# The tail of a cached attention: head 6 with V held still, head 5's sums and the last turn ahead of it, head 7 in steps

## The chip, the cores and the metric

The kernel runs on one core of a Trainium2 chip. The metric is the device time of one execution in microseconds. Times inside an execution are given in microseconds from the start of its span.

## The reference

Two layers of attention with a cached K and V, each followed by a gated feed-forward layer, for 4 sequences of one token each. The weights and the caches of both attention layers are the same; so are those of both feed-forward layers.

```python
# x [4,1,512]; k_cache, v_cache [4,8,8192,128]; wq [512,4096]; wo [4096,512]; bfloat16
def attention(x):                                   # 32 query heads over 8 K/V heads, W = 2048
    q = (x @ wq).reshape(B, 1, 32, 128).transpose(0, 2, 1, 3)
    k, v = (repeat(c[:, :, Sk - W:], 4, axis=1) for c in (k_cache, v_cache))
    p = softmax(einsum("bhqd,bhkd->bhqk", q, k) * 128 ** -0.5)
    o = einsum("bhqk,bhkd->bhqd", p, v)
    return o.transpose(0, 2, 1, 3).reshape(B, 1, 4096) @ wo
def feed_forward(x):                                # w_gate, w_up [512,1792], w_down [1792,512]
    return (sigmoid(x @ w_gate) * (x @ w_up)) @ w_down
x = x + attention(layernorm(x));  x = x + feed_forward(layernorm(x))
x = x + attention(layernorm(x));  x = x + feed_forward(layernorm(x))
```

"Head" below is one of the 8 K/V heads with its 4 query heads. Its V for the 4 sequences is 2 MB.

## The kernel before

**Plan and order.** The program is first a list of operations (`P.op`): each has an engine, an assumed duration, and tiles that it reads and writes. `_schedule` (L95) simulates all engines with those durations and picks an order for each engine; an operation's `odeps` only make it come later than certain others of its own engine in that order. SP's transfers keep the order of the list. Engines then run their lists in order, and wait on semaphores where tiles demand it. So an instruction that has to wait holds up everything behind it on its engine.

**The first half.** Attention 1 loads K and V head by head, turns K with TensorE and leaves it in SBUF (`kt`); output weights `wo` stay in `wo_sb`. A feed-forward layer follows.

**The second attention** is the loop over `HEADS2` (heads 0 to 7 in order). K lies in SBUF already; V is streamed again. `load_v` brings V of head n+2 into the place that K of head n left free, in one transfer for most heads and in three for head 7 (1 MB, 0.5 MB, 0.5 MB). Each step of the loop does `scores` for head n and then `v2_head` for head n-2 (`AHEAD = 2`); heads 6 and 7 come after the loop. For one head:

- `scores`: 16 products of q and K (L742), maximum (L751), its exchange between partitions (L755, L757, L761), exponential on ScalarE (L764), a 32x32 transpose on VectorE (L772) and the *turn*, one product with a permutation on TensorE (L775, named `PT`; the list `turns` keeps them).
- `weights`: the expansion of the turned exponentials into `pt` on VectorE (L786), the denominators (L798, L801 on VectorE, L806 on TensorE, reciprocal L811). `pt` has two halves, taken in turn.
- `pv_wo`: p times V, in one of two ways. Heads whose number is in `WIDE` take the *wide* way (`wide_pv`): pieces of `pt` are the stationary operand and V streams past in 32 products of 256 columns, four of them on different 32-column strips of the array (L827); ScalarE copies the four partial results out of PSUM (L835, named `pvc`), and matmuls in float32 add them up (L842, the head's *sums*). The others hold *V still*: 64 blocks of V of 128x128 are the stationary operand in turn, and 32 columns of `pt` stream past (L869). Then VectorE normalises (L879). For heads 0 to 6 there follow four *selection* matmuls (L905), a selection on VectorE (L912) and the head's *output projection* (L920, named `WO`), which adds into one PSUM bank over all seven heads. Head 7 has a projection of its own (L890).
- `early_residual` takes the seven heads' result out of PSUM: a cast on ScalarE (L932), the rest of it on VectorE (L935), and a turn on TensorE (L942, named `w_turn`).

In the second attention before the change, heads 0, 1 and 7 hold V still and heads 2 to 6 are wide; the exponential of head 7 is followed on ScalarE by the load of the table for the sigmoid (L766).

**The last feed-forward layer** (`glu`) has the layer norm, gate and up products (L1004), the sigmoid and the down-projection (56 products, L1072), whose result is copied (L1085) and sent out. Its weights are the last transfers of SP's list.

Of the kernel before, what the change touches and what calls it, by code (L numbers as in the profile page):

```python
# [267 lines left out]
def build(nc, A_x, A_k, A_v, A_wq, A_wo, B_wg, B_wu, B_wd, out):  # L268
# [4 lines left out]
    _, HKV, SK, DH = A_k.shape  # L273
# [28 lines left out]
    KLEAD = 3  # L302
    AHEAD = 2
    NWR = 7
    WIDE = {0: {0: 4, 1: 4, 2: 4, 3: 4, 4: 4, 5: 4, 6: 2}, 2: {2: 2, 3: 2, 4: 2, 5: 2, 6: 2}}
    HEADS1 = list(range(HKV))
    HEADS2 = list(range(HKV))

# [27 lines left out]
    with es:  # L336
# [54 lines left out]
        P = _Plan()  # L391


        def blk_ap(s):
            return {"kt": kt, "ar": arena, "pt": pt, "pb": pb, "sx": side}[s[0]][:, s[1] * UNIT:(s[1] + s[2]) * UNIT]

        def blk_tok(s):
            return tuple((s[0], u) for u in range(s[1], s[1] + s[2]))

        def kblk(h, b):  # L400
            return ("kt", (h * NB + b) * UBLK, UBLK)
# [9 lines left out]
        def ar(u, n):  # L411
            return ("ar", u, n)

        def sx(u, n):
            return ("sx", u, n)
# [23 lines left out]
        def c_dve(n, rate=None):  # L439
            return tm["dve_fix"] + n * (tm["dve_f32"] if rate is None else rate)  # L440

        def c_act(n):
            return tm["act_fix"] + n * tm["act_el"]
# [11 lines left out]
        def load_v(L, h):  # L455

            got = []
            u0 = 0
            for s in WHERE["V%d_%d" % (L, h)]:
                n = s[2]  # L460
                dma("V%d_%d_%d" % (L, h, u0), blk_ap(s), v_d[h][:, :, u0 * UNIT:(u0 + n) * UNIT], w=blk_tok(s),
                    rate={32: "bw_16k", 16: "bw_8k"}.get(n, "bw_4k"), nbytes=128 * n * UNIT * 2)
                got.append((s, u0 * UNIT // 128))
                u0 += n
            return got
# [267 lines left out]
        def scores(L, n, h, sbk, tbk):  # L733

            k2 = n % 2

            def e_s(pe):
                last = None
                for c in range(NCH):
                    for b in range(NB):  # L740
                        q0 = (h * NB + b) * STRIP + 28 - REP * c
                        last = pe.matmul(ps[32 * b:32 * b + 32, sbk, 0:CB * 128],  # L742
                                         qs[:, q0:q0 + 32],
                                         blk_ap(kblk(h, b))[:, c * CB * 128:(c + 1) * CB * 128],
                                         start=(c == 0), stop=(c == NCH - 1), skip_group_check=True)
                return last
            kr = [t for b in range(NB) for t in blk_tok(kblk(h, b))]
            P.op("tensor", "S%d_%d" % (L, h), 16 * tm["pe_s"] * (0.55 if L == 0 else 1.0), e_s, r=kr + [("qs",)], w=[("pss", sbk)], banks=(sbk,))
            nmv = nm[:, k2:k2 + 1]
            P.op("vector", "smax%d_%d" % (L, h), c_dve(CB * 128),  # L750
                 lambda v: v.tensor_reduce(nmv, ps[:, sbk, 0:CB * 128], AXX, ALU.max, negate=True),  # L751
                 r=[("pss", sbk)], w=[("nm", k2)], banks=(sbk,))

            P.op("vector", "sadd%d_%d" % (L, h), c_dve(32),
                 lambda v: v.tensor_scalar(tin[:, :], same[:, :], nmv, None, ALU.add),  # L755
                 r=[("nm", k2), ("same",)], w=[("tin",)])
            P.op("vector", "strn%d_%d" % (L, h), c_dve(32), lambda v: v.transpose(tout[:, :], tin[:, :]),  # L757
                 r=[("tin",)], w=[("tout",)])
            gv = nmg[:, k2:k2 + 1]
            P.op("vector", "smin%d_%d" % (L, h), c_dve(32),  # L760
                 lambda v: v.tensor_reduce(gv, tout[:, :], AXX, ALU.min), r=[("tout",)], w=[("nmg", k2)])  # L761
            zv = zz[:, k2:k2 + 1]
            def e_exp(a):
                o = a.activation(pbuf[:, :], ps[:, sbk, 0:CB * 128], ACTF.Exp, bias=gv, scale=1.0, accum_out=zv)  # L764
                if n == HKV - 1:
                    a.preload_act_table_set("sigmoid_and_others")  # L766
                return o
            P.op("scalar", "sexp%d_%d" % (L, h), c_act(CB * 128) + 200.0, e_exp,
                 r=[("pss", sbk), ("nmg", k2)], w=[("pb", 0), ("pb", 1), ("z", k2)], banks=(sbk,))


            P.op("vector", "ptr%d_%d" % (L, h), 650.0, lambda v: v.transpose(turned[:, :], pbuf[:, :]),  # L772
                 r=[("pb", 0), ("pb", 1)], w=[("pb", 2), ("pb", 3)])
            return P.op("tensor", "PT%d_%d" % (L, h), 270.0,
                 lambda pe: pe.matmul(ps[:, tbk, 0:CB * NQ].rearrange("p (j x) -> p j x", x=NCH * REP), perm[:, :],  # L775
                                      turned[:, :].rearrange("p (j x) -> p j x", x=32)[:, :, 0:NCH * REP],
                                      start=True, stop=True, skip_group_check=True),
                 r=[("pb", 2), ("pb", 3), ("perm",)], w=[("pspt", tbk)], banks=(tbk,))
# [70 lines left out]
        def pv_wo(L, n, h, pbk, pieces, prev=()):  # L849
            k2 = n % 2  # L850
            kp = n % NPT
            wide = WIDE[L].get(n, 0)
            obk = pbk[k2] if L else 6 if wide else 5
# [73 lines left out]
        def early_residual(L):  # L927


            hi, lo = pb[:, 0:D], pb[:, D:2 * D]  # L930
            tk = [("psw", n) for n in range(NWR)]
            P.op("scalar", "w_hi%d" % L, c_act(D), lambda a: a.copy(hi, ps[:, WB, 0:D]), r=tk, w=[("pb", 0), ("pb", 1)],  # L932
                 banks=(WB,))
            P.op("vector", "w_lo%d" % L, c_dve(D),
                 lambda v: v.tensor_tensor(lo, ps[:, WB, 0:D], hi, ALU.subtract),  # L935
                 r=tk + [("pb", 0), ("pb", 1)], w=[("pb", 2), ("pb", 3)], banks=(WB,))

            def e_turn(pe):
                last = None
                for c in range(NC):  # L940
                    for i, part in enumerate((hi, lo)):
                        last = pe.matmul(ps[:, MB, c * NB:(c + 1) * NB], part[:, c * 128:(c + 1) * 128], ofbb[:, :],  # L942
                                         start=(c == 0 and i == 0), stop=(i == 1), skip_group_check=True)
                return last
            P.op("tensor", "w_turn%d" % L, 8 * tm["pe_pair"], e_turn,
                 r=[("pb", u) for u in range(4)] + [("ofbb",)], w=[("pswt",)], banks=(MB,))
            P.op("vector", "w_early%d" % L, c_dve(NX),
                 lambda v: v.tensor_tensor(xT[:, :], ps[:, MB, 0:NX], xT[:, :], ALU.add),
                 r=[("pswt",), ("xT",)], w=[("xT",)], banks=(MB,))
# [144 lines left out]
        def eyes(L, at, kinds):  # L1094

            got, a0 = {}, 0
            for wide in kinds:
                rows = NR * wide
                e_ = blk_ap(at)[:, a0:a0 + 2 * rows].bitcast(F32)
                P.op("vector", "eye%d_%d" % (L, rows), c_dve(128),  # L1100
                     lambda v, e_=e_, rows=rows: v.tensor_reduce(
                         e_, ident_b[:, :].rearrange("p (q y) -> p y q", y=rows), AXX, ALU.add),
                     r=[("ident_b",)], w=list(blk_tok(at)) if a0 == 0 else [("eye", L, rows)])
                got[wide] = e_
                a0 += 2 * rows
            SUMS[L, "eye"] = (tuple(blk_tok(at)) + tuple(("eye", L, NR * w_) for w_ in kinds[1:]), got)

        layer_norm(0, SCALE)
        eyes(0, ar(40, 1), sorted(set(WIDE[0].values())))

# [54 lines left out]
        vs2 = {}  # L1165
        SB2, TB2 = [3, 0], [1, 2]

        def v2_head(n):
            h = HEADS2[n]
            if n == min(WIDE[2], default=-1):  # L1170
                eyes(2, sx(20, 1), sorted(set(WIDE[2].values())))
            if n == NWR:
                early_residual(2)
            pv_wo(2, n, h, (5, 6), vs2[h], turns[n + 1:n + 2])

        for n in range(2):
            vs2[HEADS2[n]] = load_v(2, HEADS2[n])
        turns = []
        for n, h in enumerate(HEADS2):
            turns.append(scores(2, n, h, SB2[n % 2], TB2[n % 2]))  # L1180
            if n + 2 < HKV:
                vs2[HEADS2[n + 2]] = load_v(2, HEADS2[n + 2])
            if n >= AHEAD:
                v2_head(n - AHEAD)
            weights(2, n, h, TB2[n % 2])
        for n in range(HKV - AHEAD, HKV):
            v2_head(n)
# [62 lines left out]
```

## Time and profile before

| | us |
|---|---|
| median of 3 runs (lowest to highest) | 180.2 (179.79 to 180.32) |
| the profiled execution: its own time | 179.77 |
| its span | 177.7 |
| TensorE busy, weight loads | 130.0, 94.6 |
| VectorE, ScalarE, GpSimd busy | 104.4, 64.4, 6.5 |
| 70.31 MB of transfers, mean rate over the span | 396 GB/s |
| mean granted TensorE clock | 0.831 of full |
| last of K's scores (L742, head 7) ends | 152.37 |
| head 5's products (L827) | 153.76 to 154.82 |
| V of head 6 lands | 158.40 |
| head 6's products (L827) | 158.44 to 160.20 |
| head 6's output projection (L920) starts | 164.73 |
| x after the second attention (L542) | 167.66 |
| down-projection (L1072) starts | 173.51 |

The columns of a view are named ahead of it. PE is TensorE, PEld its weight loads (which overlap with products), DVE VectorE, ACT ScalarE, POOL GpSimd, SP the engine that issues transfers; a "q" behind an engine's name is its sequencer. "x" is a count. A name such as `ps<-kt,pt` gives what is written and what is read; in `128*32 128x256` the first pair is rows and columns of the array that the stationary operand fills, the second the operand that streams past. Brackets at a line's end hold the idle time of the engine ahead of it and what ended it. The busy time of TensorE in products is modelled at their ends.

### The profile page before, as it was taken

What the parts mean: (1) busy time and instruction counts of PE and PEld (TensorE: products, weight loads), DVE (VectorE), ACT (ScalarE), POOL (GpSimd) and SP (SyncE); (2) the same over time, 40 slices, a digit from 0 to 9 for tenths busy, and PEclk for the clock granted to TensorE, in tenths of its full rate; (3) what the DMA queues carried; (4) which work ended last, traced back from release to release, by engine and by line L of the source; (5) the groups of instructions that cost most, each with busy time, mean ns of one, the idle gap of its engine ahead of it and who ended that gap; (6) DMA issues with size and microseconds to landing.
All of it is one profiled execution on the core that took longest, in us unless ns stands there. A gap on an engine that the chain in (4) does not pass through costs nothing.

```text
span 177.7 us, 4796 instructions
## 1 busy us (share of the span) xinstructions
PE 130.0 (73%) x2139; PEld 94.6 (53%) x2139; DVE 104.4 (59%) x271; ACT 64.4 (36%) x94; POOL 6.5 (4%) x16
## 2 busy tenths in 40 slices
PE   0494399898895986968867767658757966748883
PEld 0382198666482663745735457648215744436673
DVE  7443016989668385786767452113599997834440
ACT  2073207966385571875642510300031132150100
POOL 5200000000000000000000001002000000000020
PEclk9999657999999999999999555555699999985555
DMA  5999999999999999999999999999999999999940
GB/s 196 420 419 424 422 443 417 435 409 437 420 424 420 423 432 424 420 428 410 422 432 388 405 407 404 368 366 410 418 445 420 424 435 428 422 407 405 411 178 5
DMA packets 10369, 70.31 MB, mean 396 GB/s; under 512 B 1129, under 2 KB 1901, under 8 KB 6893
## 3 DMA queue, kind: packets, MB, share of 16 engines
q1 hardware_dynamic: 10340, 70.00, 95.3%
q8 instruction: 17, 0.28, 0.6%
q14 instruction: 4, 0.02, 0.0%
q10 hardware_dynamic: 8, 0.00, 0.0%
HBM read 70.00 MB, written 0.00 MB: 394 GB/s over the span
## 4 chain that ended last, share of the span: by engine, by line
DMA 59%; PE 17%; DVE 9%; SPq 6%; issue 4%; ACT 3%; POOLq 1%; POOL 0%; ACTq 0%; DVEq 0%
DMA arena<-in_A_v_cache_dram 43%; DMA kt<-in_A_v_cache_dram 12%; SPq L448 6%; DMA arena<-in_A_wq_dram 5%; PE ps L827 4%; PE ps L742 2%; PE ps L1004 2%; DVE pt L786 2%; PE ps L842 2%; ACT pb L764 1%; DVE nmz L751 1%; PE ps L869 1%; PE ps L1072 1%; PE ps L920 1%; DVE pb L772 1%
## 5 line engine op out<-in xcount | busy, mean ns | idle before, releaser
L729 ACT COPY kt<-ps 128x1024 bf16<-128x1024 bf16 x40 | 39.5, 1013 | 22.1 <-PE ps L719 21.8
L719 PE MATMUL ps<-ident_r,kt 128*128 128x128 bf16 x512 | 38.6, 232 | 3.4 <-DMA kt<-in_A_k_cache_dram 2.7
L719 PEld LDWEIGHTS ps<-ident_r,kt 128*128 128x128 bf16 x512 | 33.2, 106 | 10.4 <-issue 3.3
L729 DVE COPY kt<-ps 128x1024 bf16<-128x1024 bf16 x24 | 29.2, 1217 | 10.2 <-PE ps L719 10.2
L764 ACT ACTIVATE pb<-ps,nmz 128x512 bf16<-128x512 f32 x16 | 11.0, 689 | 36.2 <-DVE nmz L761 36.2
L786 DVE TENSOR_TENSOR pt<-ps,ofbr 128x1024 bf16<-128x1024 f32 x16 | 19.4, 1212 | 2.6 <-PE ps L775 2.6
L742 PE MATMUL ps<-kt,qs 128*32 128x512 bf16 x256 | 17.9, 407 | 4.1 <-ACT pb L764 2.8
L772 DVE STREAM_TRANSPOSE pb<-pb 128x512 bf16<-128x512 bf16 x16 | 11.3, 705 | 13.1 <-ACT pb L764 13.0
L827 PE MATMUL ps<-arena,pt 128*64 128x512 bf16 (+1 forms) x128 | 13.4, 391 | 7.0 <-DMA arena<-in_A_v_cache_dram 7.0
L751 DVE TENSOR_REDUCE nmz<-ps 128x1 f32<-128x512 f32 x16 | 10.9, 683 | 4.4 <-PE ps L742 4.4
L827 PEld LDWEIGHTS ps<-arena,pt 128*64 128x64 bf16 (+1 forms) x128 | 6.0, 117 | 12.3 <-DMA arena<-in_A_v_cache_dram 8.3
L742 PEld LDWEIGHTS ps<-kt,qs 128*32 128x32 bf16 x256 | 5.9, 101 | 10.5 <-ACT pb L764 3.6
L835 ACT COPY arena<-ps 128x512 f32<-128x512 f32 (+1 forms) x7 | 3.9, 556 | 13.4 <-PE ps L827 13.4
L842 PE MATMUL ps<-arena 128*128 128x16 f32 x52 | 7.3, 272 | 1.7 <-ACT arena L835 1.2
L612 POOL TENSOR_TENSOR rs<-pt,rs 128x4 f32<-128x4 f32 x4 | 4.0, 1012 | 120.3 <-DVE pt L608 120.3
L1004 PE MATMUL ps<-xn,arena 128*128 128x5 bf16 (+1 forms) x210 | 7.6, 172 | 0.8 <-DVE pt L600 0.6
L1004 PEld LDWEIGHTS ps<-xn,arena 128*128 128x128 bf16 x210 | 7.7, 118 | 1.0 <-issue 0.6
L842 PEld LDWEIGHTS ps<-arena 128*128 128x128 f32 x52 | 6.7, 201 | 2.5 <-ACT arena L835 2.5
L920 PE MATMUL ps<-wo_sb,onr 128*16 128x512 bf16 x56 | 6.4, 445 | 1.7 <-DVE onr L912 1.7
L827 PE MATMUL ps<-kt,pt 128*32 128x256 bf16 x160 | 6.0, 298 | 1.9 <-DMA kt<-in_A_v_cache_dram 1.9
L660 DVE TENSOR_TENSOR qs<-ps,rs 128x64 bf16<-128x64 f32 x2 | 0.4, 220 | 10.0 <-PE ps L650 10.0
L775 PE MATMUL ps<-pb,perm 128*128 128x256 bf16 x16 | 4.7, 293 | 1.9 <-DVE pb L772 1.8
(122 smaller groups left out, 144.2 us busy)
## 6 DMA issues: line engine op xcount, KB each, us to landing
kt<-in_A_k_cache_dram SPq DMA_DIRECT2D x8, 2048.0 KB, 24.5
arena<-in_A_v_cache_dram SPq DMA_DIRECT2D x7, 2048.0 KB, 20.1
kt<-in_A_v_cache_dram SPq DMA_DIRECT2D x5, 2048.0 KB, 18.0
wo_sb<-in_A_wo_dram SPq DMA_DIRECT2D x8, 512.0 KB, 25.1
arena<-in_B_w_gate_dram SPq DMA_DIRECT2D x6, 448.0 KB, 7.8
arena<-in_B_w_up_dram SPq DMA_DIRECT2D x5, 448.0 KB, 6.9
kt<-in_A_wq_dram SPq DMA_DIRECT2D x2, 1024.0 KB, 10.0
arena<-in_B_w_down_dram SPq DMA_DIRECT2D x4, 512.0 KB, 13.4
```

Source lines behind the costliest of these rows:

```text
L448: o = P.op("sync", name, 0.0, lambda e, dst=dst, src=src: e.dma_start(dst, src), r=r, w=w, dma_bytes=nbytes, dma_rate=tm[rate])
L719: last = pe.transpose(bankb(bank)[:, (v * NB + q) * 128:(v * NB + q + 1) * 128], kt[:, c0:c0 + 128], ident_b[:, :])
L729: return (e.tensor_copy if ev == "vector" else e.copy)(to, fr)
L742: last = pe.matmul(ps[32 * b:32 * b + 32, sbk, 0:CB * 128], qs[:, q0:q0 + 32], blk_ap(kblk(h, b))[:, c * CB * 128:(c + 1) * CB * 128], sta ...
L751: lambda v: v.tensor_reduce(nmv, ps[:, sbk, 0:CB * 128], AXX, ALU.max, negate=True),
L764: o = a.activation(pbuf[:, :], ps[:, sbk, 0:CB * 128], ACTF.Exp, bias=gv, scale=1.0, accum_out=zv)
L772: P.op("vector", "ptr%d_%d" % (L, h), 650.0, lambda v: v.transpose(turned[:, :], pbuf[:, :]), r=[("pb", 0), ("pb", 1)], w=[("pb", 2), ("pb ...
L786: lambda v: v.tensor_tensor(ptv.rearrange("p (j b r) -> p j b r", b=NB, r=REP), ps[:, tbk, 0:CB * NQ].rearrange("p (j r) -> p j r", r=REP) ...
L827: last = pe.matmul(ps[rows * g:rows * (g + 1), bank, 0:wide * 128].rearrange("p (c d) -> p c d", c=wide), pt[:, w0:w0 + rows], v, start=(i ...
L842: last = pe.matmul(ps[:, out[0], out[1]:out[1] + NR], part[:, c * 128:(c + 1) * 128], ey[wide][:, c * NR:(c + 1) * NR], start=(c == 0), st ...
L920: last = pe.matmul(ps[32 * j:32 * j + NR, WB, 0:D], onr[:, j * NR:(j + 1) * NR], wo_sb[:, h * WOH + j * D:h * WOH + (j + 1) * D], start=(n ...
L1004: last = pe.matmul(ps[:, bank, fc * wid:(fc + 1) * wid], cols[:, fc - g0, :], xn[:, ktc * (NB + 1):ktc * (NB + 1) + wid], start=(ktc == 0 ...
```

## The change

Head 6 leaves `WIDE` and so holds V still. Three lists are kept beside the loop: `turns` as before, `exps` (the exponential of each head) and `worked` (the output projection of the head handled last). With them, four orders are added:

- head 7's exponential comes after head 5's `pvc` on ScalarE;
- head 6's products come after head 5's output projection on TensorE, and after the last turn as before;
- of head 7's three pieces, the first comes after head 6's selection matmuls and the second after head 6's output projection;
- head 7's own projection comes after `w_turn`.

```diff
-    WIDE = {0: {0: 4, 1: 4, 2: 4, 3: 4, 4: 4, 5: 4, 6: 2}, 2: {2: 2, 3: 2, 4: 2, 5: 2, 6: 2}}
+    WIDE = {0: {0: 4, 1: 4, 2: 4, 3: 4, 4: 4, 5: 4, 6: 2}, 2: {2: 2, 3: 2, 4: 2, 5: 2}}
...
             if n == NWR:
                 early_residual(2)
-            pv_wo(2, n, h, (5, 6), vs2[h], turns[n + 1:n + 2])
+            n0 = len(P.ops)
+            pv_wo(2, n, h, (5, 6), vs2[h], turns[n + 1:n + 2] + worked if n == HKV - AHEAD else turns[n + 1:n + 2])
+            new = P.ops[n0:]
+            worked[:] = [o for o in new if o.name.startswith("WO")]
+            if n == HKV - AHEAD - 1:
+                exps[-1].odeps.update(o for o in new if o.name.startswith("pvc"))
+            if n == HKV - 1:
+                mine = [o for o in new if o.name.startswith(("PV", "WO"))]
+                for name, o in (("sel2_%d" % HEADS2[n - 1], mine[0]), ("WO2_%d" % HEADS2[n - 1], mine[1]), ("w_turn2", mine[-1])):
+                    o.odeps.update(p for p in P.ops if p.name == name)
...
-        turns = []
+        turns, exps, worked = [], [], []
         for n, h in enumerate(HEADS2):
             turns.append(scores(2, n, h, SB2[n % 2], TB2[n % 2]))
+            exps.append(P.ops[-3])
```

The order that results at the end of the second attention, on TensorE from head 4's output projection on:

| before | after |
|---|---|
| products of head 6 (32 wide) | sums of head 5 |
| last turn | last turn |
| sums of head 5 | selection of head 5 |
| sums of head 6 | output projection of head 5 |
| selection of head 5, denominators of head 7 | denominators of head 7 |
| selection of head 6 | products of head 6 (64, V still) |
| output projection of head 5 | selection of head 6 |
| products of head 7, first half | products of head 7, first half |
| output projection of head 6 | output projection of head 6 |
| products of head 7, second half | products of head 7, second half |
| `w_turn`, projection of head 7 | `w_turn`, projection of head 7 |

On VectorE, behind the transpose L772 of head 7: before, L798 and L801, the expansion L786, then L879 of heads 5 and 6, L912 of head 5, L811, L912 of head 6; after, L879 of head 5, L798, the expansion L786, L912 of head 5, L801, L811, L879 and L912 of head 6. The orders on SP and GpSimd are the same.

## The prediction

> **What bounds the kernel now.** I read the slices of the page first, then the chain of waits from 150 us on, the timeline around the changed steps, the windows of TensorE's clock, the source view of the narrow products, and the DMA issues. The slices give busy tenths in 40 equal parts of the span (4.44 us each):
>
> ```profile
> PE   0494399898895986968867767658757966748883
> PEclk9999657999999999999999555555699999985555
> DMA  5999999999999999999999999999999999999940
> ```
>
> The transfers never pause until slice 38, so nothing that ends inside the stream is worth time by itself. What counts is what ends after the stream: slices 38 and 39. The chain (start us, us, what) says which work that is:
>
> ```profile
> 137.76 20.64 DMA kt<-in_A_v_cache_dram
> 158.44 1.76 PE ps L827 x32
> 160.21 0.33 PE ps L775
> 160.53 0.68 PE ps L842 x4
> 161.24 0.38 ACT side L835
> 161.66 1.05 PE ps L842 x4
> 162.74 0.21 DVE onb L879
> ...
> 163.83 0.97 PE ps L869 x32
> 164.80 0.56 PE ps L920 x3
> 165.39 0.59 ACT pb L932
> ...
> 167.66 0.19 DVE xn L542
> ```
>
> From the landing of head 6's V at 158.40 on, the chain holds no transfer: it is compute alone, down to the output at 175.24. Head 6's wide products come first (L827), then three pieces of older work that stand in TensorE's queue behind them: the last turn (L775), head 5's sums (first L842), and only then head 6's sums (second L842). The timeline shows why head 5's sums are so late:
>
> ```profile
> 156.84 1.28 ACT L766 ACT_TABLE_LOAD   x1
> 158.14 0.37 ACT L835 COPY side<-ps 128x256 f32<-128x256 f32 x1
> 160.57 1.23 DVE L786 TENSOR_TENSOR pt<-ps,ofbr 128x1024 bf16<-128x1024 f32 x1 [2.62 <-PE ps L775]
> 163.76 1.03 PE L869 MATMUL ps<-pt,kt 128*128 128x32 bf16 x32
> ```
>
> The 158.14 copy is head 5's; its products ended at 154.82, but it stood behind the last exponential and the table load. TensorE meanwhile sat idle, and its clock was halved just as the last stretch began (columns: busy and count of PE, PEld, DVE, ACT, POOL, then PEclk, DMA share, GB/s):
>
> ```profile
> 157.00:158.00 1.00, 0.00 (x0) 0.00 (x0) 0.92 (x3) 1.00 (x1) 0.00 (x0) 1.00 1.01 422
> 159.00:160.00 1.00, 1.00 (x24) 0.59 (x16) 0.00 (x0) 0.00 (x0) 0.00 (x0) 0.50 1.03 418
> ```
>
> **The change, part by part**, on the clock of the profiled execution (span 177.7, its own time 179.77, so 2.07 outside the span; the median of the runs is 180.2, 0.43 above it). Per engine the order of instructions is unchanged up to head 4's output projection on TensorE (ends 156.53). No transfer is moved: SP issues the same list, its last weight load at 158.45, and GpSimd's list is unchanged.
>
> Head 5's copy before the last exponential: it may run at 154.87 to 155.24 (0.37). The exponential waits for L761 until 155.95 and started at 156.05, so the move costs nothing while those 0.7 us of cover last, 0.37 if they did not.
>
> Head 5's sums before the last turn: 156.53 to 157.05 (0.52, the 153.31 row at full clock). The turn waits for VectorE's transpose, which ends 157.57. Free, and the 0.68 after 160.53 goes.
>
> The last turn: 157.62 to 157.90 (0.28, as at 153.19) instead of 160.14. VectorE takes head 5's normalising (0.18) behind the transpose, then the expansion L786 at 157.93 to 159.15 (1.23), and only then head 5's selection L912, 159.06 to 159.27. This is the added wait. Head 5's output projection (L920) needs that selection: 159.32. Behind it in TensorE's queue stand the last denominators (L806) and all of head 6's products. A projection at half clock holds the next matmul 0.53 (163.23 to 163.76), the denominators another 0.14 (140.28 to 140.42). So head 6's products start at 159.32 + 0.53 + 0.14 = 159.99, 1.55 later than before, though V landed at 158.40.
>
> Head 6 with V still: 32 wide products (1.76), a copy (0.38) and its sums (1.05) go; 64 narrow ones come. Their row:
>
> ```profile
> L869 PEld LDWEIGHTS ps<-pt,kt x64: 103/104/115, 163.8 to 166.1; 128*128 128x128 bf16 x64
> L869 PE MATMUL ps<-pt,kt x64: 187/188/208, 163.8 to 166.1; 128*128 128x32 bf16 x64
> ```
>
> 32 of them took 1.03 with 0.188 for one, hence (1.03 - 0.188)/31 = 27 ns apart at half clock; at full clock (38 in 1.10, one 0.176) 25 ns. So 64 take 0.188 + 63 x 0.027 = 1.90: they end at 161.89. Normalising (0.04 to start, 0.18) ends 162.11; the selection matmuls start 162.16 and hold the next 0.24 (162.99 to 163.23): head 7's first half starts 162.40 (its V landed at 142.82 + 18.1 = 160.92), and head 6's projection 0.97 later, 163.37; before it was 164.73. VectorE's selection for it is done by 162.8. The sum is **164.73 - 163.37 = 1.36 us**.
>
> Behind it nothing changes shape: cast L932, difference L935, turn L942, head 7's projection L890, x at about 166.3. Head 7's second half starts at 163.9; its last V piece landed at 144.05 + 19.4 = 163.45 and is needed at 164.3, a cover of 0.85. The turn ahead of head 7's projection is the order they already had. The layer norm, GLU and down-projection move up whole: the down-projection would start at 172.15, and its four weights landed at 169.1, 170.4, 171.6 and
>
> ```profile
> arena<-in_B_w_down_dram SPq DMA_DIRECT2D x1, 256.0 KB, 13.8
> ```
>
> that is 158.45 + 13.8 = 172.25, needed by the last 8 of 56 products, near 173.4. So the whole 1.36 reaches the end.
>
> One correction. The clock changed at 18.69, 28.93, 97.19, 127.91 and 158.63 us: the distances are 3, 20, 9 and 9 times 3.413 us, so it is decided on a fixed raster whose phase each run draws anew. The window that ended at 158.63 held 0.94 us of PE busy. Other phases put the fall anywhere from about 157 to 160.2. Later than 158.6 it favours the kernel before: with its wide products at 1.06 (row 153.76) instead of 1.76 and head 5's sums at 0.52, it wins up to 1.05, the changed kernel only some 0.25 (one projection), because the narrow products hardly feel the clock. The gain is then 0.56 to 1.36 over the late half of the phases and about 1.3 over the early half. I take **1.2 us**: 180.2 - 1.2 = 179.0 (178.6 on the profiled execution's own time).
>
> **The rivals.** *The clock stays up* (faster still). The steps pulled forward fill the idle stretch from 156.5 to 158.4: sums 0.52, turn 0.28, selection 0.3. PE busy in that window would rise from 0.94 to about 1.8; the window from 127.92 had 1.74 and kept the clock. Then everything after runs at full clock and only the last weights bound the end: last products at about 172.6 rather than 175.2, a gain of 2.6, so 177.6. Against it: the window from 93.79 held 2.38 busy and still lost the clock, so busy time is not what is counted, and these steps are short streams of 16 columns. The Trainium skill, "TensorE: Matmul & The Clock Gate", section "The HAM clock gate", has a free-running window of about 3.4 us and lets an idle one halve the clock; the raster here agrees (3.413 us), but the window that lost it was not idle. By that rule, taken strictly, this rival would win.
>
> *The fall comes late in the usual run of before* (slower). If the clock held until 162.05, the wide path would put head 6's projection at about 162.8, ending 163.2, against 163.97 for the changed kernel at half clock: its start on the narrow products comes 1.5 late and is not won back. It is 0.6 to 0.8 slower: about 180.8. It decides once before keeps full clock past about 161.5. Against it: such a run of before would be some 2 us shorter than the profiled one, while the timed runs lie at 179.79 to 180.32 around 179.77.
>
> *Weight loads do not hide behind the narrow products* (slower). Each of the 64 loads takes 104 ns; end to end they would be 6.7 instead of 1.90, 4.8 more: 180.2 - 1.2 + 4.8 = 183.8. It decides from a spacing of about 27 + 1360/64 = 48 ns. The row of head 7 speaks against it: 27 ns apart, with the same shape, in the same place. The Trainium skill, "TensorE: Matmul & The Clock Gate", section "Packing small matmuls", says that a load overlaps with matmuls in flight only where its row group differs, which speaks against V held still, since all these loads fill all 128 rows; the trace here does not agree, 32 pairs of 104 and 188 ns having taken 1.03 us.
>
> *A transfer ends last* (no change). If the runs' transfers end later than the profile's by some 2.4 us, the last weights bound both kernels and the reordering is hidden: 179.9 to 180.4. The median's 0.43 above the profile is for it; that the weights lay ready before 173.5 is against it. Between 1.2 and 2.4 later it hides part.
>
> **How the numbers follow.** A difference of about 0.3%, 0.54 us, is what a measurement of this kernel can tell from none. Forecast, a gain of 0.6 to 1.7 (178.5 to 179.6): 0.68. Clock stays up (177.6): 0.06. Transfers hide it (179.9 to 180.4): 0.12. Late fall (180.8): 0.11. Loads bare (183.8): 0.03. Faster is 0.68 + 0.06 = 0.74, same 0.12, slower 0.14. The range takes in the forecast and the no-change case, and at the low end 0.3 us more for narrow products at 25 ns and a projection at full clock: 178.2 to 180.4.
>
> **What the next profile would show.** Right: head 5's copy near 154.9 ahead of the exponential; its sums near 156.5; 64 narrow products starting near 160.0, not at V's landing, ending near 161.9; head 6's projection near 163.4; x near 166.3; the clock at half from about 158.6. Wrong would be: narrow products more than 35 ns apart, a wait for V of head 7 at 163 to 165, a wait for down-projection weights after 172, or full clock beyond 162 in either kernel.

## The result, and the profile after

The changed kernel takes 178.75 us (median of 6 runs, 178.44 to 179.13); before takes 180.25 beside it (6 runs, 179.79 to 180.58). The ratio is 0.9922 with a 95% interval of 0.9902 to 0.9941: 1.1 to 1.8 us less. The forecast was 179.0, or 1.2 us less. The profiled execution took 178.58, with a span of 176.6.

The chain of waits after (start us, us, what), from head 7's exponential to x:

```profile
156.45 0.79 ACT pb L764 x2
157.26 0.72 DVE pb L772
158.03 0.30 PE ps L775
158.35 1.22 DVE pt L786
159.57 0.14 DVE onr L912
159.76 0.61 PE ps L920 x3
160.37 0.15 PE ps L806 x2
160.52 1.74 PE ps L869 x64
162.28 0.20 DVE onb L879
...
162.84 0.87 PE ps L869 x32
163.71 0.56 PE ps L920 x4
164.30 0.59 ACT pb L932
...
166.56 0.19 DVE xn L542
```

Before, the chain came out of a transfer at 158.40. Now no transfer is on it: head 6's V is there, and its 64 products stand behind the last turn, the expansion (L786), head 5's selection and projection. Between them and head 6's projection (163.64) stand the normalising, head 6's selection and the first half of head 7; the copy and the two rounds of sums that stood there before are gone. The timeline shows head 5's copy and sums where the change put them, in time in which TensorE had waited:

```profile
155.34 0.37 ACT L835 COPY side<-ps 128x256 f32<-128x256 f32 x1 [2.48 <-PE ps L827]
...
156.92 0.62 PE L842 MATMUL ps<-side 128*128 128x16 f32 x4
...
160.38 1.87 PE L869 MATMUL ps<-pt,kt 128*128 128x32 bf16 x64
```

One thing moves against the change in this execution: at 131.82 to 135.24 the clock was halved for one stretch of the raster, in a part that is the same in both kernels, and everything behind it is 0.4 later than in the profile of before (the last exponential at 156.45 instead of 156.05). Measured from that exponential, head 6's projection comes 7.19 us after it instead of 8.68: 1.49 less.

### The profile page after: what moved, and what is told of

The parts are those of the page before. It is cut to its first block, busy times and chain, and to the rows that moved or that the text cites. A ratio compares the mean times of both kernels' runs of the same rounds, so it can differ in the third digit from the quotient of the medians.

```text
span 176.6 us, 4850 instructions
## 1 busy us (share of the span) xinstructions
PE 129.3 (73%) x2167; PEld 94.5 (53%) x2167; DVE 104.7 (59%) x271; ACT 64.2 (36%) x93; POOL 6.5 (4%) x16
## 4 chain that ended last, share of the span: by engine, by line
DMA 52%; DVE 18%; PE 18%; ACT 5%; issue 3%; SPq 2%; POOLq 1%; POOL 0%; ACTq 0%; DVEq 0%
DMA arena<-in_A_v_cache_dram 31%; DMA kt<-in_A_k_cache_dram 11%; DVE pt L786 5%; DMA arena<-in_A_wq_dram 5%; DMA arena<-in_B_w_up_dram 4%; PE ps L719 4%; PE ps L827 4%; PE ps L742 3%; ACT pb L764 3%; DVE pb L772 3%; DVE nmz L751 2%; PE ps L869 2%; SPq L448 2%; DVE tout L757 1%; PE ps L1072 1%
## 5 line engine op out<-in xcount | busy, mean ns | idle before, releaser
L719 PE MATMUL ps<-ident_r,kt 128*128 128x128 bf16 x512 | 39.4, 235 | 4.4 <-DMA kt<-in_A_k_cache_dram 3.7
L719 PEld LDWEIGHTS ps<-ident_r,kt 128*128 128x128 bf16 x512 | 33.8, 107 | 11.5 <-DMA kt<-in_A_k_cache_dram 4.1
L742 PE MATMUL ps<-kt,qs 128*32 128x512 bf16 x256 | 19.0, 427 | 3.8 <-ACT pb L764 2.5
L786 DVE TENSOR_TENSOR pt<-ps,ofbr 128x1024 bf16<-128x1024 f32 x16 | 19.4, 1215 | 0.2 <-PE ps L775 0.2
L772 DVE STREAM_TRANSPOSE pb<-pb 128x512 bf16<-128x512 bf16 x16 | 11.3, 709 | 13.1 <-ACT pb L764 13.0
L827 PE MATMUL ps<-arena,pt 128*64 128x512 bf16 (+1 forms) x128 | 12.6, 355 | 7.1 <-DMA arena<-in_A_v_cache_dram 7.1
L842 PE MATMUL ps<-arena 128*128 128x16 f32 x52 | 7.2, 269 | 2.7 <-ACT arena L835 2.2
L842 PEld LDWEIGHTS ps<-arena 128*128 128x128 f32 x52 | 6.6, 197 | 3.5 <-ACT arena L835 3.5
L561 PE MATMUL ps<-pt,nmz 128*128 128x4 f32 x12 | 3.5, 362 | 3.4 <-DVE pt L583 2.5
L806 PE MATMUL ps<-zd,rqb 128*128 128x16 bf16 x32 | 3.3, 176 | 3.4 <-DVE pt L786 3.3
```

What stands on the lines that cost most here:

```text
L719: last = pe.transpose(bankb(bank)[:, (v * NB + q) * 128:(v * NB + q + 1) * 128], kt[:, c0:c0 + 128], ident_b[:, :])
L742: last = pe.matmul(ps[32 * b:32 * b + 32, sbk, 0:CB * 128], qs[:, q0:q0 + 32], blk_ap(kblk(h, b))[:, c * CB * 128:(c + 1) * CB * 128], sta ...
L786: lambda v: v.tensor_tensor(ptv.rearrange("p (j b r) -> p j b r", b=NB, r=REP), ps[:, tbk, 0:CB * NQ].rearrange("p (j r) -> p j r", r=REP) ...
L827: last = pe.matmul(ps[rows * g:rows * (g + 1), bank, 0:wide * 128].rearrange("p (c d) -> p c d", c=wide), pt[:, w0:w0 + rows], v, start=(i ...
L842: last = pe.matmul(ps[:, out[0], out[1]:out[1] + NR], part[:, c * 128:(c + 1) * 128], ey[wide][:, c * NR:(c + 1) * NR], start=(c == 0), st ...
```

## The experiments

They ran in turns with the kernel before, in three groups (e1 to e4, e5 to e8, e9 to e11), each group on a chip of its own. The ratio is to before; it is not exactly the ratio of the two medians. Before, head 6's projection starts 8.68 us behind head 7's last exponential, after it 7.19; I give this distance for each, because it leaves out shifts that come from earlier stages (it still depends on when the clock fell in that one execution: for e10 the clock was full from 155.49 to 165.73, so that its 5.21 cannot be set beside e3's 6.33).

| run | median us | before | ratio (95%) | exponential to head 6's projection |
|---|---|---|---|---|
| e1: orders, head 6 wide | 179.18 | 180.07 | 0.9943 (0.9915 to 0.9970) | 7.63 |
| e2: still alone | 178.92 | 180.07 | 0.9948 (0.9925 to 0.9972) | 7.48 |
| e3: products not held behind projection | 177.99 | 180.07 | 0.9895 (0.9864 to 0.9927) | 6.33 |
| e4: selection first | 178.32 | 180.07 | 0.9913 (0.9882 to 0.9944) | 6.67 |
| e5: copy not first | 180.32 | 179.97 | 1.0039 (1.0014 to 1.0065) | 8.89 |
| e6: no steps | 178.62 | 179.97 | 0.9938 (0.9911 to 0.9964) | 7.07 |
| e7: before with filler | 178.66 | 179.97 | 0.9933 (0.9905 to 0.9960) | 6.59 |
| e8: after with filler | 178.25 | 179.97 | 0.9920 (0.9895 to 0.9946) | 6.77 |
| e9: after again | 179.02 | 180.09 | 0.9945 (0.9925 to 0.9965) | 6.93 |
| e10: as e3, again | 178.48 | 180.09 | 0.9903 (0.9872 to 0.9935) | 5.21 |
| e11: as e3, last piece split | 177.86 | 180.09 | 0.9880 (0.9846 to 0.9913) | 6.20 |

**e1, the orders with head 6 still wide.** The changed kernel with

```diff
-    WIDE = {0: {0: 4, 1: 4, 2: 4, 3: 4, 4: 4, 5: 4, 6: 2}, 2: {2: 2, 3: 2, 4: 2, 5: 2}}
+    WIDE = {0: {0: 4, 1: 4, 2: 4, 3: 4, 4: 4, 5: 4, 6: 2}, 2: {2: 2, 3: 2, 4: 2, 5: 2, 6: 2}}
```

> All the added orders, but head 6 stays wide (its wide products cannot be held behind head 5's projection, so they start at the landing of V). Theory A (work queued between V's landing and head 6's projection is what the change shortens): head 5's copy leaves ScalarE early, its sums (0.68 us after the landing in the trace of before) lie before the landing, and head 6's copy no longer waits for them; head 6's sums start near 160.7 instead of 161.66, its projection near 163.7 instead of 164.73: about 1.0 us less than before, 179.2. Rival B (holding V still is what gains, since the copy and the float32 sums of head 6 go): no gain, 180.2. Rival C (filling TensorE's idle stretch keeps its clock up): full clock in the tail and up to 2.6 us less, 177.6.

1.0 us less, as theory A has it. The timeline of TensorE:

```profile
159.01 1.17 PE L827 MATMUL ps<-kt,pt 128*32 128x256 bf16 x32 [1.93 <-DMA kt<-in_A_v_cache_dram]
160.11 0.39 PE L775 MATMUL ps<-pb,perm 128*128 128x256 bf16 x1
...
160.65 1.03 PE L842 MATMUL ps<-side 128*128 128x16 f32 x4
...
163.62 0.60 PE L920 MATMUL ps<-wo_sb,onr 128*16 128x512 bf16 x4
```

Behind the landing there is one round of sums (L842) instead of two. So most of the gain can be had without holding V still; the runs do not tell e1 from the changed kernel. In this execution the clock fell only at 159.82, so its wide products took 1.17 instead of 1.76 and part of what the trace shows is that.

**e2, V still and no order.** The kernel before with the first line of the change alone.

> Only head 6 leaves the wide way, none of the orders. Theory A: head 5's copy still waits behind the last exponential and the table load (158.1 to 158.5); its sums, now ahead of the last turn and of head 6's products in TensorE's queue, hold these until about 160.2; head 6's projection starts near 163.9 instead of 164.73: 0.8 us less than before, 179.4, and 0.6 more than the changed kernel. Rival B: all of the gain is here, 178.75.

0.94 us less than before; its interval overlaps the changed kernel's. By the times alone rival B is not excluded: its 178.75 is nearer to the median than theory A's 179.4, and e9 below, the changed kernel again, gains no more (0.9945). Against B stand e1, which gained with head 6 wide, and the trace: head 5's sums came at 159.10, after a wait for the copy, and held up the rest until 160.57, as theory A says.

```profile
159.10 1.03 PE L842 MATMUL ps<-side 128*128 128x16 f32 x4 [2.03 <-ACT side L835]
...
160.57 1.87 PE L869 MATMUL ps<-pt,kt 128*128 128x32 bf16 x64
```

Either half thus gives about 1 us, and both together 1.4 in the first comparison and 1.0 in the second (e9), less than the 2.0 of the halves added: the two seem to take away the same wait in part. That both give more than either alone is not shown.

**e3 and e10, head 6's products not behind head 5's projection.** The changed kernel with

```diff
-            pv_wo(2, n, h, (5, 6), vs2[h], turns[n + 1:n + 2] + worked if n == HKV - AHEAD else turns[n + 1:n + 2])
+            pv_wo(2, n, h, (5, 6), vs2[h], turns[n + 1:n + 2])
```

> The changed kernel without one of its orders: head 6's products need not come after head 5's projection; they then stand right behind the last turn and head 5's selection. Theory A (in the changed kernel these products wait for VectorE's expansion, 1.5 us after V landed): they start at the landing, near 158.4 on the scale of before; head 6's projection near 162.1; the landing of head 7's last piece (163.45) is the next bound, x near 165.0 instead of 166.1: 1.1 us less than the changed kernel, 177.6. Rival: V of head 6 or 7, or the last weights (172.25), bound the tail already, so nothing is won, 178.7.

> The changed kernel without the order of head 6's products behind head 5's projection, again: 0.5 to 1.1 us less than the changed kernel on the same chip. Rival (the earlier difference was the spread of the runs): within 0.3 of it.

0.9895 and 0.9903 of before; on the same chip as the second, the changed kernel (e9) had 0.9945:

> The changed kernel again, unaltered, to stand on one chip beside the two that follow: about 1.4 us less than before, 178.7.

The difference of e9 and e10 is 0.0042 of 180 us, 0.8 us (0.5 by the medians), inside what was expected, but the two intervals still overlap a little (0.9925 to 0.9965 and 0.9872 to 0.9935). TensorE's timeline of e3 shows the wait gone, and the next one:

```profile
159.36 1.89 PE L869 MATMUL ps<-pt,kt 128*128 128x32 bf16 x64 [0.75 <-DMA kt<-in_A_v_cache_dram]
161.18 0.60 PE L920 MATMUL ps<-wo_sb,onr 128*16 128x512 bf16 x4
...
162.87 0.60 PE L920 MATMUL ps<-wo_sb,onr 128*16 128x512 bf16 x4
...
164.42 0.56 PE L869 MATMUL ps<-pt,kt 128*128 128x32 bf16 x16 [0.41 <-DMA kt<-in_A_v_cache_dram]
```

The products start at V's landing, head 5's projection follows them, and the last 16 products of head 7 wait for its last piece. Of the four orders that the change adds, this one seems to be a cost.

**e4, head 5's selection ahead of the expansion.** The changed kernel with, behind the loop,

```diff
+for o in P.ops:
+    if o.name == "ptx2_7":
+        o.odeps.update(p for p in P.ops if p.name in ("osel2_5",))
```

> The changed kernel with one order more: on VectorE head 5's selection comes ahead of the expansion for head 7, so that head 5's projection can run near 158.4 instead of 159.3, and head 6's products start near 158.9 to 159.0 instead of 160.0. Theory A: again bounded by head 7's last piece at 163.45; about 1.0 us less than the changed kernel, 177.7. Rival as for the run without the order: 178.7. A second rival: the expansion, 0.4 later, becomes the wait of head 7's products; it is not needed before 161, so no cost is expected.

178.32, ratio 0.9913: the direction expected, between theory A's 177.7 and its rival's 178.7, with a size that the runs cannot tell from none against the changed kernel (intervals overlap). Its runs spread from 177.18 to 179.82, and the profiled one is the longest: there the clock fell at 151.58 and stayed at half to the end (e10's fell at 152.08 but came back at 155.49), and head 5's wide products took 1.90 (155.06 to 156.96) instead of 1.06.

**e5, the copy not ahead of the exponential.** The changed kernel without `exps[-1].odeps.update(...)`.

> The changed kernel without one order: head 5's copy may stay behind head 7's exponential and the table load on ScalarE. Theory A: the copy then ends near 158.5, head 5's sums near 159.5, the last turn near 159.9, the expansion near 161.1; head 5's projection, and with it head 6's products that are ordered behind it, start near 161.4 and 162.0 instead of 159.3 and 160.0: 1.5 to 2 us more than the changed kernel, 180.2 to 180.8, no gain or a loss against before. Rival: the copy is a detail and the gain stays, 178.8.

180.32: 0.3 to 1.2 us *more* than before. The timeline has the chain that was expected, each step 0.6 to 1 later on the clock of this execution:

```profile
159.12 0.37 ACT L835 COPY side<-ps 128x256 f32<-128x256 f32 x1
...
159.55 0.88 PE L842 MATMUL ps<-side 128*128 128x16 f32 x4 [2.03 <-ACT side L835]
...
160.68 1.22 DVE L786 TENSOR_TENSOR pt<-ps,ofbr 128x1024 bf16<-128x1024 f32 x1
...
161.82 0.21 DVE L912 TENSOR_TENSOR onr<-ps,ofbr 128x64 bf16<-128x64 f32 x1
...
162.11 0.60 PE L920 MATMUL ps<-wo_sb,onr 128*16 128x512 bf16 x4
```

So the orders on TensorE pay with the copy early and not with it late. With it late, e2 gained and e5 lost; beyond e2, e5 has the order of head 6's products behind head 5's projection and the steps of head 7, and e6, which follows, shows no effect of the steps. That points to that order as what turns the change into a loss.

**e6, without the steps of head 7.** The changed kernel without the block under `if n == HKV - 1`.

> The changed kernel without the orders on head 7's pieces and on its projection: three quarters of head 7's products then precede head 6's projection, whose cast and difference therefore start about 0.3 later, but head 7's own projection runs before the turn instead of behind it, which takes 0.3 to 0.5 off the end. Theory A: within 0.4 of the changed kernel, 178.4 to 179.1. Rival: the steps carry a good part of the gain, 179.4 or more.

178.62 and 0.9938, no different from the changed kernel (0.9922 and 0.9945). Head 6's projection ended 163.90 and head 7's own was over at 165.24, before the turn ended at 165.74. Neither a gain nor a loss by the steps shows.

**e7 and e8, a filler for the clock.** Products of `ident_b` with `wo_sb[:, 0:512]` into a PSUM bank that is not in use, whose results nobody reads:

```diff
+            def e_warm(pe):
+                for _ in range(count):
+                    last = pe.matmul(ps[:, MB, 0:512], ident_b[:, :], wo_sb[:, 0:512], start=True, stop=True,
+                                     skip_group_check=True)
+                return last
...
```

In e7, 7 of them behind head 4's projection in the kernel *before*; in e8, 2 there and 5 behind head 5's selection in the changed one. All other orders are as they were.

> The kernel before, with 7 products of 128x512 that nobody reads put on TensorE into its idle stretch from 156.5 to 158.4 (1.5 us at full clock, into a PSUM bank that is free then); all else as before. Theory on the clock: the window keeps enough streaming that the clock stays full over the landing, head 6's wide products take 1.06 instead of 1.76 and head 5's and head 6's sums 0.5 instead of 0.9 to 1.0 each: 0.6 to 1.9 us less than before, about 179. Rival: the clock is not worth that, 180.1; if the clock falls before the filler it takes 3 us and delays head 6 by 1, 181.

> The changed kernel with the same kind of filler, 2 products of 128x512 behind head 4's projection and 5 behind head 5's selection (0.4 and 1.1 us at full clock, both in stretches where TensorE waits); all else as in the changed kernel. Theory on the clock: the narrow products are 27 ns apart at half and 25 at full clock and head 5's projection 0.60 or 0.39, so at most 0.3 us less than the changed kernel: 178.4 to 178.8. Rival from the prediction (with the clock up only the last weights bound the tail): up to 1.4 us less, 177.4.

e7 came to 178.66, 0.9933: added work that does nothing took 0.7 to 1.7 us off the kernel before, as much as the change does. Its timeline (the filler, and head 6's wide products at full clock):

```profile
157.37 1.68 PE L1171 MATMUL ps<-wo_sb,ident_r 128*128 128x512 bf16 x7
...
158.99 1.06 PE L827 MATMUL ps<-kt,pt 128*32 128x256 bf16 x32
```

The clock fell only at 163.10. e8 kept it until 165.66 and had 0.9920, not told apart from the changed kernel without a filler; its 64 products took 1.75 us instead of 1.87. So the changed tail hardly feels the clock, and the rival's further 1.4 us are not there: x was earlier (165.60), but the down-projection paused after its first 15 products with no wait that the profile shows:

```profile
171.71 0.61 PE L1072 MATMUL ps<-arena,pt 128*25 128x128 bf16 x15 [0.86 <-DVE pt L1044]
172.75 0.69 PE L1072 MATMUL ps<-arena,pt 128*25 128x128 bf16 x17 [0.43 <-issue]
```

What held it for 0.43 us is open; the second of its weights landed at 154.44 + 16.2 = 170.6. In this execution the time that was won ahead of the down-projection was lost again inside it.

**e11, the last piece of V in two.** As e3, with

```diff
-                                  for u, n in (((0, 16), (16, 8), (24, 8)) if h == HKV - 1 else ((0, UHEAD),))]
+                                  for u, n in (((0, 16), (16, 8), (24, 4), (28, 4)) if h == HKV - 1 else ((0, UHEAD),))]
```

> As the run before it, and head 7's last piece of V (8 units of 256 columns) comes in two transfers of 4 units. If the landing of that piece is now what starts the end (16 products, 0.56 us, ran behind it), half of them move ahead of it: 0.2 to 0.3 us less than without the split. Rival: one more transfer with shorter rows costs as much in the stream: no difference or 0.2 more.

177.86, 0.9880 (0.9846 to 0.9913): 2.2 us less than before, and its interval lies wholly below that of the changed kernel on the same chip (0.9925 to 0.9965). It beats both kernels on that chip; the changed kernel's first interval (0.9902 to 0.9941) it overlaps. That the split itself adds anything to e10 is not shown, since these two intervals overlap.

## Why the prediction was right, point by point

**The head of the queue.** Predicted: head 5's sums at 0.48 behind the last exponential's start, head 6's products at 3.94 behind it. Measured: 156.92 and 160.38 less 156.45, that is 0.47 and 3.93. The added wait for the expansion and for head 5's projection was costed as it is, with two small errors that cancel: the projection started 3.31 behind the exponential instead of 3.27, and it and the denominators held the products 0.62 instead of 0.67.

**The narrow products.** Predicted 1.90 for 64, measured 1.87; 27 ns apart. The rival with loads in the open (6.7 us) is out. The statement of the Trainium skill, "TensorE: Matmul & The Clock Gate", section "Packing small matmuls", that a load overlaps with matmuls in flight only where its row group differs, does not hold for these: 64 loads of 104 ns went by in 1.87 us. (The same section also lets a load into the background weight buffer be pulled ahead; no run here shows which of its ways was taken.)

**Two terms a little too large.** The hold of the selection matmuls was taken as 0.24, from a row in which a projection followed, and measured 0.16 where products of V follow (162.53 to 162.69); head 7's first half held 0.95 instead of 0.97. With the 0.03 of the narrow products this is the step from the 1.36 of the sum to the 1.49 of the trace.

**The correction for the clock.** The forecast took 0.16 off for the clock's phase. The two comparisons of the changed kernel with before give 1.4 us (0.9922) and 1.0 (0.9945): 1.2 is between them, so the size is right as far as the runs can tell, but they do not tell it from the uncorrected 1.36 either. That the profiled execution took 178.58 against the 178.6 forecast for it is luck: 1.49 was won in the tail, and 0.4 was lost to the stretch at 131.82, which the forecast did not have. The reasoning was too narrow: I let the fall lie between 157 and 160.2. The traces have it at 151.58 (e4), 152.08 (e10) and 161.24 (e9), a fall at 131.82 that the trace of before had not shown, and clocks that came back inside the tail (e6 at 162.58, e3 at 164.20, and also in e2, e5, e9 and e11). One of the signs that I had named for being wrong, full clock beyond 162 in either kernel, is among them: in e9 the changed kernel had full clock from 164.65 to 168.07, behind head 6's projection, and the forecast held all the same.

**The rival "clock stays up".** It was rightly given little. The window before the fall held 1.69 us of PE busy in the changed kernel against 0.94 before, and the clock fell all the same, as the streams of 16 columns let expect:

```profile
155.72:159.13 3.41, 1.69 (x19) 1.18 (x19) 2.60 (x10) 2.06 (x3) 0.00 (x0) 1.00 0.99 411
```

**The rival "the fall comes late".** The size of what before wins by a high clock was right (e7's projection at 6.59 behind the exponential, against about 6.75 as I had it). What was wrong is the other side: I kept the changed kernel at half clock there. With both clocks high (e7, e8) the two stand at 178.66 and 178.25, with intervals that overlap, so even then no loss shows. My argument against this rival, that no run of before was that short, rested on three runs: of the 79 that stand beside the experiments, five took 178.22 to 178.85, 0.9 to 1.6 less than the profiled one. Where the clock fell in those is not known.

**Transfers.** Predicted: cover of 0.85 for head 7's last piece of V and of 1.15 for the last weights (172.25, needed near 173.4). No wait for either is in the changed kernel's chain, but the weights landed later than I had them, at 158.91 + 14.0 = 172.91, and were needed at 173.63: a cover of 0.7. e3, e10 and e11 use the first cover up. In e10 and e11 the second is gone as well: the last 8 products start at 172.26 and 172.56, behind weights that landed at 158.43 + 13.8 = 172.23 and 159.50 + 13.0 = 172.50. A further gain in this tail is likely to need these transfers earlier.

## What to carry to other kernels

When a queue in order holds short old steps behind work that waits for a transfer, move them ahead of the transfer's landing, but follow what each of them waits for on the other engines: here the early copy on ScalarE made it pay, and one order too many seems to have cost 0.5 to 0.8 us of it. Before reordering a tail that runs at half clock, try a filler in the idle stretch ahead of it; it costs one edit and here was worth as much as the reordering. Cost steps from rows of the same shape at the same clock, and count what holds the next instruction, not how long the last one lasts.

## What the runs showed of the hardware that was not expected

The clock's raster of 3.413 us holds in all 13 traces of this case, but the busy time of TensorE does not say whether a window keeps it: 2.95 us lost it in e7 (159.68 to 163.10), and 1.74 kept it in the profile of before. An estimate that fits better, worked out from the products' shapes in these traces: columns streamed, at 0.417 ns each (half of what 32 columns, 26.7 ns apart, take at half clock; the filler's 512 columns, 0.216 us apart in e7, give 0.42), times the share of the array's columns that the stationary operand fills, with float32 columns counted four times. From 17 us on, no window at full clock with more than 1.33 us of it lost the clock and none with less than 1.17 kept it; between, both occur. (With float32 counted once the two figures are 1.24 and 1.09.) That window of e7 has 0.85 of it and that of before 1.17; the 1.69 us of short streams in the changed kernel have 0.39, and the 7 filler products (512 columns, 128 of 128 filled) 1.5. The measure was fitted afterwards to 13 executions of nearly the same program, so it is no more than an estimate.
